# The leading expert is chosen four units early, half of its w1 is loaded during attention, and the gap between attention and experts is reordered

## The chip, the cores and the metric

The kernel runs on one NeuronCore of a Trainium2 chip. Its time is the device time of one execution in microseconds; the figure that counts is the median of the runs shown. The engines are called PE (TensorE), DVE (VectorE), ACT (ScalarE), POOL (GpSimd) and SP (SyncE, which mainly issues DMAs). Each engine works through its own instructions in order.

## The reference

Three stages follow each other. The first is a gated linear attention over 4 batches, 8 heads, 768 positions and 48 columns a head: `state = f * state + k v`, `y = q state`, with `f = sigmoid(f_logit)`. The second is a mixture of 8 experts with one expert a token; the third is a gated two-matrix product and two more matrices.

```python
# x: 3072 tokens x 384, from the attention
xn = x / (norm(x) + 1e-6);  en = emb / (norm(emb) + 1e-6)
logits = xn @ en.T / tau
expert_idx = argmax(logits, axis=1)
gate_w = softmax(logits)[arange(N), expert_idx]
for e in range(8):
    mask = expert_idx == e
    out[mask] = gate_w[mask, None] * (relu(x[mask] @ w1[e]) @ w2[e])   # w1[e] 384x1024, w2[e] 1024x384
# then
h = (out @ g1) * (out @ g2) @ g3
return h @ g_out
```

## The kernel before

**Attention and routing.** The 3072 tokens are 24 units of 128 (6 chunks of 4 batches). Attention is a software pipeline over units, written out by hand in the list `parts` (from L748), and each engine executes its instructions in the order in which the program states them. For each unit `s_xt` makes the token-major output and partial logits on PE, `s_sq` the sum of squares on ACT, `s_lg` (L534) the logits on DVE. `route(u0, n)` (L571) routes n units: GpSimd takes a power for the norm (L582), DVE finds the expert of each token (L583 to L594), PE counts its rank among that expert's tokens (matmuls L599 to L602, with the running counts `base`), DVE makes the row to write to (L612), the norm and the softmax denominator (L613 to L622), and GpSimd scatters each unit with one indirect DMA (L626) into `xsd`, 3072 rows for each expert. Route calls cover 6, 6, 4 and 4 units during attention (the list `routing`), then three (`pre`) and one (`last`) behind it.

**Choosing the order of experts.** `finish_route()` (L635, called `ends`) runs after all 24 units: PE sums the counts (`cnt`, L642) and a flag (`ok`, L643), and DVE ranks the experts by count (L651 to L677). Slot 0 is the expert with the most tokens. The results are `slot_e` (the expert of each slot), `slot_r` (its row in `xsd`) and `offs` (its columns in the result). SyncE reads `slot_e` and `slot_r` into registers to address loads. Slot by slot the matmuls have the fixed widths 448, 428, 416, 404, 396, 388, 384 and 376 columns.

**The gap.** Behind the attention loop comes a stretch (L790 to L833) in which the last two units and the routing end on DVE, while PE gets other work: part of the product of g3 and g_out for the third stage. `w3_turn(i)` transposes a tile of g3 on PE (L166), ACT and DVE evacuate it into two parts (L168, L169); `w3_times(i)` makes 24 products of 384 columns (L177) in four steps of six, and ACT and DVE copy the result out (L180, L181). `turn_w` and `times_w` hold four such tiles as generators, and `step(gen, n)` issues their next n steps, so the order of the calls in the gap is the order on every engine.

**The experts.** A phase is half an expert: half of w1 (768 KB) and half of w2. `prefetch(ph)` loads both into the two `stg` buffers (L306), whose memory attention used before, and lists their splits (ACT L134, GpSimd or DVE L135: upper and lower part) for `wsplit`. In phase 0 the w1 half is loaded on SyncE's queue, the w2 half on ScalarE's. `xs_load(0)` (L848) gathers the rows of slot 0 after the last scatter, `xs_gate` scales them with the gate (L865 on DVE, L867 on ACT), `xs_prep` transposes them (L876), and `g1_step` and `g2_step` are the expert's matmuls (L889, `hb`, and L903, `acc`), the first of which ends the gap. The third stage (L985, L998) follows when the experts are done.

Of the kernel before, what the change touches and what calls it, by code (L numbers as in the profile page):

```python
# [19 lines left out]
def attn_moe_glu_kernel(  # L20
# [61 lines left out]
    slot_r = const.tile([P, E], I32, name="slot_r")  # L82
    didx = const.tile([P, NU], I32, name="didx")
# [11 lines left out]
    cvw = [None]  # L95

# [205 lines left out]
    def fetch(ph, src, shape, q=SP):  # L302
        h = ring[ph % 2].tile(shape, F32R, tag="wh", name="wh")
        l = ring[ph % 2].tile(shape, F32R, tag="wl", name="wl")
        t = stage[0].tile(shape, F32, tag="stg", name="stg")
        q.dma_start(out=t, in_=src)  # L306
# [7 lines left out]
    def phase_src(ph, i, q):  # L314
# [4 lines left out]
        e = q.value_load(slot_e[0:1, n:n + 1], min_val=0, max_val=E - 1)  # L319
# [7 lines left out]
    def prefetch(ph):  # L327
        ta, ga = fetch(ph, phase_src(ph, 0, SP), [P, KD, 512])
        wsplit.add(ga)
        yield  # L330

        q = SP if ph else A
        tb, gb = fetch(ph, phase_src(ph, 1, q), [P, 4, DM] if ph < 2 * E else [P, KD, 512], q)
        phases[ph] = (ta, tb)
        wsplit.add(gb)
# [231 lines left out]
    def route(u0, n):  # L567
# [12 lines left out]
        pi = t1("pi", I32)  # L580
# [53 lines left out]

    def finish_route():  # L635
# [5 lines left out]
        b, b2 = bank([P, E], "cnt"), bank([P, 1], "ok")  # L641
# [13 lines left out]
        V.tensor_tensor(out=key, in0=key, in1=num, op=ALU.subtract)  # L655
# [24 lines left out]
    with tc.manual_schedule():  # L680
# [37 lines left out]
        def constants():  # L718
            V.tensor_copy(out=num, in_=slot_e)
            for dst, a, b in ((wrev, -1.0, E), (cbase, N, 0), (base, N // P, 0)):  # L720
                V.tensor_scalar(out=dst, in0=num, scalar1=float(a), scalar2=float(b), op0=ALU.mult, op1=ALU.add)
            for e in range(E):
# [69 lines left out]
        step(routing[-1], 2)  # L792
# [5 lines left out]
        s_lg(NU - 2)  # L798
        pre = route(NU - 4, 3)
        last = route(NU - 1, 1)  # L800
        ends = finish_route()
        step(pre)
# [3 lines left out]
        step(times_w[0], 2)  # L806
        spread.append(1)
        step(pre, 7)
        s_xt(NU - 1)
        s_sq(NU - 1)  # L810
        step(times_w[0])
        s_lg(NU - 1)
# [3 lines left out]
        step(ends)  # L816
        step(last, 5)
        step(times_w[1])
        step(last)
        step(times_w[1])  # L820
        step(last)
        step(ends, 2)
        for _ in range(3):
            step(last)
            step(ends)
        step(last, 99)
        step(ends, 99)
        step(times_w[0], 9)
        step(times_w[1])
        step(turn_w[2], 9)  # L830
        step(times_w[1], 9)
        attn.close()
# [12 lines left out]
        def xs_load(e):  # L845
            r = SP.value_load(slot_r[0:1, e:e + 1], min_val=0, max_val=(E - 1) * N)
# [63 lines left out]
        step(ahead)  # L910
        xs_load(0)
        step(turn_w[3], 9)
        step(times_w[2], 2)
        wsplit.pull(3)
        step(ahead)
# [8 lines left out]
        close_w3()  # L924
# [242 lines left out]
```

## Time and profile before

| | us |
|---|---|
| median of 3 runs | 738.99 (738.5 to 739.14) |
| the profiled execution | 736.44 |
| its span, first to last instruction | 734.7 |
| TensorE busy | 717.3 |
| VectorE, ScalarE, GpSimd busy | 345.4, 337.5, 339.2 |
| mean granted TensorE clock | 0.995 of full |

The rows of the trace are timed from the start of the span of the profiled execution, which is 1.7 us shorter than that execution. Matmuls are pipelined and their ends are modelled: of a run of matmuls the start of the next thing says more than the busy time. A timeline row gives start, duration, engine, line, what is written and read, how many were merged into the row, and in brackets the idle time before it and what ended that.

### The profile page before, as it was taken

The page shows a single profiled execution, that of the slowest core. Times are in us where ns is not written, and L with a number is a line of the kernel's source. Part 1 is how long each engine was busy: PE and PEld are TensorE (multiplying, and loading weights), DVE is VectorE, ACT ScalarE, POOL GpSimd, SP SyncE. Part 2 cuts the span into 40 slices and gives each one's busy share as a digit, 9 for nine tenths or more (in the row PEclk, how much of TensorE's full clock was granted, in tenths as well). Part 3 has the DMA queues.
Part 4 walks back from the last instruction along what each step waited for, and adds up shares of the span by engine and source line. Part 5 has one row for each costly group of instructions (what it writes and reads, how often), then busy time and mean ns, then how long its engine had stood idle before and what let it go on. Part 6 is the DMA issues. An engine that isn't in the chain of part 4 may idle for free.

```text
span 734.7 us, 13343 instructions
## 1 busy us (share of the span) xinstructions
PE 717.3 (98%) x5169; PEld 657.9 (90%) x5169; DVE 345.4 (47%) x672; ACT 337.5 (46%) x703; POOL 339.2 (46%) x423
## 2 busy tenths in 40 slices
PE   8999999998999999999999999999999999999996
PEld 7999989988999899999999988988888888888885
DVE  8889999956455564345343132222322322323222
ACT  5687978844557475465554542122112122121210
POOL 5467787783977776584564852102202201221002
PEclk9999999999999999999999999999999999999998
DMA  8999999626767778645443230000100100100001
GB/s 165 237 215 222 228 249 231 168 99 189 239 195 244 217 237 259 189 145 153 133 136 106 97 86 1 22 22 1 43 1 1 43 1 1 43 1 22 22 1 46
DMA packets 132158, 86.50 MB, mean 118 GB/s; under 512 B 106481, under 2 KB 114681, under 8 KB 132089
## 3 DMA queue, kind: packets, MB, share of 16 engines
q1 hardware_dynamic: 128489, 75.34, 38.6%
q0 software_dynamic: 3072, 9.46, 3.5%
q8 instruction: 42, 0.69, 0.4%
q10 hardware_dynamic: 528, 0.79, 0.4%
q14 instruction: 27, 0.22, 0.1%
HBM read 70.57 MB, written 15.01 MB: 116 GB/s over the span
## 4 chain that ended last, share of the span: by engine, by line
PE 54%; issue 10%; DMA 5%; POOL 4%; ACT 2%; DVE 1%; SPq 1%; POOLq 0%; ACTq 0%; DVEq 0%
PE pa L985 11%; PE pb L985 11%; PE ob L998 10%; PE acc L903 9%; PE hb L889 9%; DMA stg<-in_moe_w_dram 5%; PE wpb L177 4%; POOL wl L135 1%; POOL out_dram L1005 1%; DMA gd<-gt 1%; ACT wh L134 1%; PE xb L876 1%; POOL gt L222 1%; POOL x L135 0%; PE w3b L166 0%
## 5 line engine op out<-in xcount | busy, mean ns | idle before, releaser
L135 POOL TENSOR_TENSOR wl<-stg,wh 128x384 fp32r<-128x384 f32 (+1 forms) x121 | 139.1, 1179 | 64.2 <-ACT wh L134 64.2
L988 DVE TENSOR_TENSOR a<-a,pb 128x512 f32<-128x512 f32 x48 | 33.0, 688 | 181.6 <-PE pb L985 175.5
L998 PE MATMUL ob<-wp,ab 128*128 128x384 f32 x576 | 108.2, 339 | 0.0
L998 PEld LDWEIGHTS ob<-wp,ab 128*128 128x128 f32 x576 | 102.3, 188 | 3.8
L903 PE MATMUL acc<-h,wh 128*128 128x448 f32 (+7 forms) x384 | 104.1, 351 | 1.0 <-DVE h L892 0.5
L889 PE MATMUL hb<-xT,wh 128*128 128x448 f32 (+7 forms) x384 | 102.5, 348 | 0.0
L985 PE MATMUL pa<-x,wh 128*128 128x512 f32 x288 | 90.2, 394 | 0.0
L985 PE MATMUL pb<-x,wh 128*128 128x512 f32 x288 | 89.9, 393 | 0.0
L892 DVE SCALAR_TENSOR_TENSOR h<-hb,h 128x448 fp32r<-128x448 f32 (+7 forms) x64 | 37.0, 579 | 108.6 <-ACT h L891 108.3
L987 ACT COPY a<-pa 128x512 f32<-128x512 f32 x48 | 28.2, 587 | 120.6 <-PE pa L985 120.6
L1005 POOL DMA_INDIRECT out_dram<-o,didx x24 | 23.2, 965 | 129.4 <-DVE o L1004 126.0
L135 POOL TENSOR_TENSOR x<-xd,x 128x512 fp32r<-128x512 f32 x18 | 22.8, 1293 | 120.6 <-ACT x L134 120.6
L990 ACT CAST ab<-a 128x512 fp32r<-128x512 f32 x48 | 29.8, 620 | 104.7 <-DVE a L988 104.7
L134 ACT CAST wh<-stg 128x384 fp32r<-128x384 f32 (+1 forms) x124 | 62.7, 563 | 32.5 <-DMA stg<-in_moe_w_dram 26.6
L903 PEld LDWEIGHTS acc<-h,wh 128*128 128x128 f32 x384 | 70.4, 188 | 4.3 <-ACT h L891 1.5
L889 PEld LDWEIGHTS hb<-xT,wh 128*128 128x128 f32 x384 | 70.8, 188 | 1.4
L889 PE MATMUL hb<-xT,wl 128*128 128x448 f32 (+7 forms) x192 | 66.7, 348 | 0.0
L903 PE MATMUL acc<-h,wl 128*128 128x448 f32 (+7 forms) x192 | 66.7, 347 | 0.0
L985 PEld LDWEIGHTS pb<-x,wh 128*128 128x128 f32 x288 | 54.2, 188 | 12.7
L985 PEld LDWEIGHTS pa<-x,wh 128*128 128x128 f32 x288 | 53.6, 188 | 9.2
L891 ACT ACTIVATE h<-hb 128x448 fp32r<-128x448 f32 (+7 forms) x64 | 32.4, 507 | 62.5 <-PE hb L889 61.8
L985 PE MATMUL pb<-x,wl 128*128 128x512 f32 x144 | 56.9, 395 | 0.0
(185 smaller groups left out, 1276.0 us busy)
## 6 DMA issues: line engine op xcount, KB each, us to landing
stg<-in_moe_w_dram SPq DMA_DIRECT2D x31, 768.0 KB, 5.8
raw<-in_moe_w_dram SPq DMA_DIRECT2D x28, 512.0 KB, 5.6
xs<-xsd SPq DMA_DIRECT2D x8, 675.5 KB, 7.4
q<-in_q_dram SPq DMA_DIRECT2D x24, 192.0 KB, 5.0
k<-in_k_dram SPq DMA_DIRECT2D x24, 192.0 KB, 5.2
v<-in_v_dram SPq DMA_DIRECT2D x24, 192.0 KB, 4.5
f<-in_f_logit_dram SPq DMA_DIRECT2D x23, 192.0 KB, 4.4
raw<-in_moe_w_out_dram SPq DMA_DIRECT2D x8, 384.0 KB, 4.6
```

What stands on the lines that cost most here:

```text
L134: A.copy(out=hi, in_=src)
L135: eng.tensor_tensor(out=lo, in0=src, in1=f32(hi), op=ALU.subtract)
L177: PE.matmul(out=o, lhsT=t[:, x, j, :], rhs=wo[:, y, j, :], start=(j + n == 0), stop=(j == KF - 1 and n == 2))
L889: PE.matmul(out=b, lhsT=w[x][:, kk, cs], rhs=xT[e][y][:, kk, :], start=(kk + n == 0), stop=(kk == KD - 1 and n == 2))
L891: A.activation(out=h[0], in_=b, func=AF.Relu)
L892: V.scalar_tensor_tensor(out=h[1], in0=b, scalar=0.0, in1=f32(h[0]), op0=ALU.max, op1=ALU.subtract)
L903: PE.matmul(out=acc[d], lhsT=w[x][:, s % 4, d * P:(d + 1) * P], rhs=hs[s][y], start=(s + n == 0), stop=(s == KF - 1 and n == 2))
L985: PE.matmul(out=b, lhsT=w[x][:, kk, cs], rhs=x2[n][y][:, kk, :], start=(kk + m == 0), stop=(kk == KD - 1 and m == 2))
L988: V.tensor_tensor(out=t, in0=t, in1=pb, op=ALU.mult)
L990: A.copy(out=ab[s][0], in_=t)
L998: PE.matmul(out=oacc[t], lhsT=ab[s][x][:, t * P:(t + 1) * P], rhs=wp[:, y, s, :], start=(s + m == 0), stop=(s == KF - 1 and m == 2))
L1005: ins = G.indirect_dma_start(out=out, out_offset=bass.IndirectOffsetOnAxis(ap=didx[:, j:j + 1], axis=0), in_=o, in_offset=None,)
```

## The change

- `choose()` (called `lead`) takes the counts after 20 units with one matmul and finds the expert that leads. Ten small DVE instructions write its number and its row into `first`, and `numc`, which `finish_route` now takes for ties, puts that expert into slot 0 whatever the last four units bring.
- The w1 half of phase 0 goes into a buffer of its own, `w1s`, and its load is issued as soon as `first` is there, in the middle of the gap. The w2 half of phase 0 and the gather of slot 0 are addressed from `first` too, the w2 half now on SyncE's queue.
- In `route`, `pi` has six buffers instead of two. The counts `cnt` and `ok` go to the other PSUM pool.
- The order of the gap is new: the last two scatters of `routing[-1]` stand behind the first step of `pre`; w3 products and the steps of `last` and `ends` alternate in another way; two steps of `times_w[2]` stand ahead of `turn_w[3]`.

```diff
@@ -80,6 +80,8 @@
     win = const.tile([P, E], F32, name="win")
     slot_e = const.tile([P, E], I32, name="slot_e")
     slot_r = const.tile([P, E], I32, name="slot_r")
+    numc = const.tile([P, E], F32, name="numc")
+    first = const.tile([P, 2], I32, name="first")
     didx = const.tile([P, NU], I32, name="didx")
     xsd = dram.tile([E * N, XW], F32, name="xsd")
     xg = dram.tile([N, DM], F32, name="xg")
@@ -93,6 +95,9 @@
     cv = cvx.enter_context(tc.tile_pool(name="cv", side="right", bufs=1, reuse_waits="tile"))
     wo = cv.tile([P, 2, KF, DM], F32R, name="wo")
     cvw = [None]
+    pre_pool = ExitStack()
+    early = pre_pool.enter_context(tc.tile_pool(name="early", side="right", bufs=1, reuse_waits="tile"))
+    w1s = early.tile([P, KD, 512], F32, name="w1s")
 
     def open_w3(tiles, turns):
         cvw[0] = tc.tile_pool(name="cvw", side="right", bufs=1, reuse_waits="tile")
@@ -299,11 +304,12 @@
     ring = []
     stage = []
 
-    def fetch(ph, src, shape, q=SP):
+    def fetch(ph, src, shape, q=SP, t=None):
         h = ring[ph % 2].tile(shape, F32R, tag="wh", name="wh")
         l = ring[ph % 2].tile(shape, F32R, tag="wl", name="wl")
-        t = stage[0].tile(shape, F32, tag="stg", name="stg")
-        q.dma_start(out=t, in_=src)
+        if t is None:
+            t = stage[0].tile(shape, F32, tag="stg", name="stg")
+            q.dma_start(out=t, in_=src)
 
         def gen():
             for i in range(shape[1]):
@@ -316,7 +322,7 @@
         half_f = slice(hf * 512, (hf + 1) * 512)
         if n == E:
             return gd[i][:, half_f].rearrange("(k p) f -> p k f", p=P)
-        e = q.value_load(slot_e[0:1, n:n + 1], min_val=0, max_val=E - 1)
+        e = q.value_load(slot_e[0:1, n:n + 1] if n else first[0:1, 0:1], min_val=0, max_val=E - 1)
         if i == 0:
             return w1[bass.ds(e, 1), :, half_f].rearrange("o (k p) f -> p (o k) f", p=P)
         return w2[bass.ds(e, 1), half_f, :].rearrange("o (k p) d -> p (o k) d", p=P)
@@ -325,12 +331,10 @@
     wsplit = Background()
 
     def prefetch(ph):
-        ta, ga = fetch(ph, phase_src(ph, 0, SP), [P, KD, 512])
+        ta, ga = fetch(ph, phase_src(ph, 0, SP), [P, KD, 512]) if ph else fetch(0, None, [P, KD, 512], t=w1s)
         wsplit.add(ga)
         yield
-
-        q = SP if ph else A
-        tb, gb = fetch(ph, phase_src(ph, 1, q), [P, 4, DM] if ph < 2 * E else [P, KD, 512], q)
+        tb, gb = fetch(ph, phase_src(ph, 1, SP), [P, 4, DM] if ph < 2 * E else [P, KD, 512])
         phases[ph] = (ta, tb)
         wsplit.add(gb)
 
@@ -577,7 +581,7 @@
         r0, rinv = t1("r0"), t1("rinv")
         nb = rt.tile([P, E], F32, name="nb", bufs=2)
         t, sm = t8("t"), t1("sm")
-        pi = t1("pi", I32)
+        pi = rt.tile([P, 8], I32, name="pi", bufs=6)[:, 0:n]
         flat = lambda a: a.rearrange("p g e -> p (g e)")
         G.tensor_tensor(out=r0, in0=ssq[:, us], in1=half[:, 0:1].to_broadcast([P, n]), op=ALU.pow)
         V.tensor_reduce(out=mx, in_=L, axis=AX.X, op=ALU.max)
@@ -632,13 +636,36 @@
             scatters.append(ins)
             G.memset(half[:, 1:2], 0.0)
 
+    def choose():
+
+
+        b = bank([P, E], "lead", "acc")
+        PE.matmul(out=b, lhsT=ones, rhs=base)
+        yield
+        key, hot, t = [rt.tile([P, E], F32, name=n) for n in ("lkey", "lhot", "lt")]
+        s = rt.tile([P, 2], F32, name="ls")
+        V.scalar_tensor_tensor(out=key, in0=b, scalar=float(E), in1=numc, op0=ALU.mult, op1=ALU.subtract)
+        yield
+        V.tensor_reduce(out=s[:, 0:1], in_=key, axis=AX.X, op=ALU.max)
+        yield
+        V.tensor_scalar(out=hot, in0=key, scalar1=s[:, 0:1], scalar2=None, op0=ALU.is_equal)
+        yield
+        V.tensor_tensor(out=t, in0=hot, in1=num, op=ALU.mult)
+        V.tensor_scalar(out=hot, in0=hot, scalar1=float(2 * E * N), scalar2=None, op0=ALU.mult)
+        yield
+        V.tensor_reduce(out=s[:, 1:2], in_=t, axis=AX.X, op=ALU.add)
+        V.tensor_tensor(out=numc, in0=num, in1=hot, op=ALU.subtract)
+        yield
+        V.tensor_copy(out=first[:, 0:1], in_=s[:, 1:2])
+        V.tensor_scalar(out=first[:, 1:2], in0=s[:, 1:2], scalar1=float(N), scalar2=None, op0=ALU.mult)
+
     def finish_route():
         okb = rt.tile([P, 1], BF16, name="okb")
         low = rt.tile([P, 1], F32, name="low")
         V.tensor_reduce(out=low, in_=pend.rearrange("p u j -> p (u j)"), axis=AX.X, op=ALU.min)
         V.tensor_scalar(out=okb, in0=low, scalar1=1e-18, scalar2=None, op0=ALU.is_ge)
         yield
-        b, b2 = bank([P, E], "cnt"), bank([P, 1], "ok")
+        b, b2 = bank([P, E], "cnt", "acc"), bank([P, 1], "ok", "acc")
         PE.matmul(out=b, lhsT=ones, rhs=base)
         PE.matmul(out=b2, lhsT=ones, rhs=okb)
         yield
@@ -652,7 +679,7 @@
         yield
         V.tensor_scalar(out=key, in0=cnt, scalar1=float(E), scalar2=None, op0=ALU.mult)
         yield
-        V.tensor_tensor(out=key, in0=key, in1=num, op=ALU.subtract)
+        V.tensor_tensor(out=key, in0=key, in1=numc, op=ALU.subtract)
         yield
         V.tensor_tensor(out=gt, in0=rows(key), in1=cols(key), op=ALU.is_gt)
         yield
@@ -719,6 +746,7 @@
             V.tensor_copy(out=num, in_=slot_e)
             for dst, a, b in ((wrev, -1.0, E), (cbase, N, 0), (base, N // P, 0)):
                 V.tensor_scalar(out=dst, in0=num, scalar1=float(a), scalar2=float(b), op0=ALU.mult, op1=ALU.add)
+            V.tensor_scalar(out=numc, in0=num, scalar1=float(E * N + 1), scalar2=None, op0=ALU.mult)
             for e in range(E):
                 G.memset(win[:, e:e + 1], float(WIN[e]))
 
@@ -789,46 +817,62 @@
                 step(turn_w[i - NU], 2)
         for gen in routing[:-1]:
             step(gen, 99)
-        step(routing[-1], 2)
         s_xt(NU - 2)
         s_sq(NU - 2)
         step(times_w[0])
         s_inter(NU - 1)
         s_out(NU - 1)
         s_lg(NU - 2)
+        lead = choose()
         pre = route(NU - 4, 3)
         last = route(NU - 1, 1)
         ends = finish_route()
+        step(lead)
         step(pre)
         step(routing[-1], 99)
         spread.append(0)
         step(pre, 6)
-        step(times_w[0], 2)
+        step(times_w[0])
         spread.append(1)
-        step(pre, 7)
+        step(pre)
+        step(lead, 3)
+        step(pre)
         s_xt(NU - 1)
         s_sq(NU - 1)
         step(times_w[0])
+        step(lead)
+        step(pre)
+        step(lead)
+        step(pre)
+        step(lead, 9)
+        step(pre)
+        SP.dma_start(out=w1s, in_=phase_src(0, 0, SP))
+        step(pre)
         s_lg(NU - 1)
         step(last)
         step(pre, 99)
         spread.append(0)
-        step(ends)
         step(last, 5)
-        step(times_w[1])
+        step(times_w[0])
         step(last)
-        step(times_w[1])
-        step(last)
-        step(ends, 2)
-        for _ in range(3):
-            step(last)
-            step(ends)
-        step(last, 99)
-        step(ends, 99)
         step(times_w[0], 9)
         step(times_w[1])
+        step(ends)
+        step(last)
+        step(ends)
+        step(last)
+        step(turn_w[2])
+        for _ in range(2):
+            step(ends)
+            step(last)
+        step(times_w[1])
+        step(ends)
+        step(last, 99)
         step(turn_w[2], 9)
+        step(times_w[1], 2)
+        step(ends, 3)
         step(times_w[1], 9)
+        step(ends, 99)
         attn.close()
         open_psum(5, 3)
 
@@ -843,7 +887,7 @@
         ids_of = {}
 
         def xs_load(e):
-            r = SP.value_load(slot_r[0:1, e:e + 1], min_val=0, max_val=(E - 1) * N)
+            r = SP.value_load(slot_r[0:1, e:e + 1] if e else first[0:1, 1:2], min_val=0, max_val=(E - 1) * N)
             xst[e] = m1p.tile([CAP // 4, 4, XW], F32, name="xs")
             SP.dma_start(out=xst[e], in_=xsd[bass.ds(r, CAP), :].rearrange("(p c) w -> p c w", c=4))
 
@@ -907,12 +951,11 @@
                     V.tensor_copy(out=xd[:, d, bass.ds(o, WIN[e])], in_=acc[d])
 
         ahead = prefetch(0)
-        step(ahead)
+        step(ahead, 2)
         xs_load(0)
+        step(times_w[2], 2)
         step(turn_w[3], 9)
-        step(times_w[2], 2)
         wsplit.pull(3)
-        step(ahead)
         step(times_w[2], 9)
         for c in range(4):
             xs_gate(0, c)
@@ -922,6 +965,7 @@
         wsplit.pull(2)
         step(prefetch(1), 2)
         close_w3()
+        pre_pool.close()
         xd = moe.enter_context(tc.tile_pool(name="xd", reuse_waits="tile", bufs=1)).tile([P, KD, DENSE], F32, name="xd")
         open_w3(2, 1)
         bg.add(late())
```

## Rows read from the trace of the kernel before

**Rows 1.** The page: busy us (share of span) of each engine.
```profile
PE 717.3 (98%) x5169; PEld 657.9 (90%) x5169; DVE 345.4 (47%) x672; ACT 337.5 (46%) x703; POOL 339.2 (46%) x423
```

**Rows 2.** TensorE's waits, 181 to 734 us: total, times, longest.
```profile
PE acc L903 <- DVE h L892: 0.5, 3, 0.2
PE acc L903 <- ACT h L891: 0.4, 1, 0.4
```

**Rows 3.** TensorE's waits in the gap, 150 to 185 us.
```profile
PE w3b L166 <- DVE w3t L169: 2.2, 1, 2.2
PE rk L599 <- DVE oh L592: 0.8, 1, 0.8
PE wpb L177 <- DVE wp L181: 0.4, 1, 0.4
```

**Rows 4.** Timeline of TensorE, 150 to 200 us.
```profile
155.37 2.36 PE L177 MATMUL wpb<-wo,w3t 128*128 128x384 f32 x12
157.66 0.93 PE L524 MATMUL xl<-sel,yT 128*64 128x104 f32 x16
158.53 2.37 PE L177 MATMUL wpb<-wo,w3t 128*128 128x384 f32 x12
161.66 0.18 PE L599 MATMUL rk<-oh,tri 128*128 128x8 bf16 x1 [0.76 <-DVE oh L592]
...
168.79 0.66 PE L166 MATMUL w3b<-ident,g 128*128 128x128 f32 x4 [2.21 <-DVE w3t L169]
169.85 8.10 PE L177 MATMUL wpb<-wo,w3t 128*128 128x384 f32 x36 [0.41 <-DVE wp L181]
177.79 1.31 PE L876 MATMUL xb<-ident,xs 112*128 112x112 f32 x12
...
181.04 0.57 PE L889 MATMUL hb<-xT,wh 128*128 128x448 f32 x2
```

**Rows 5.** Stretches of 0.5 us; PEclk is the first figure after the engines.
```profile
170.00:170.50 0.50, 0.50 (x3) 0.50 (x4) 0.50 (x2) 0.07 (x1) 0.00 (x0) 0.79 0.94 332
...
171.00:171.50 0.50, 0.50 (x3) 0.50 (x2) 0.00 (x0) 0.00 (x0) 0.00 (x0) 0.50 1.06 414
...
173.50:174.00 0.50, 0.50 (x4) 0.50 (x4) 0.00 (x0) 0.50 (x2) 0.31 (x1) 0.80 0.74 173
```

**Rows 6.** Timeline of VectorE, 143 to 161 and 160 to 200 us.
```profile
158.84 0.17 DVE L613 TENSOR_SCALAR r<-r 128x3 f32<-128x3 f32 x1 [2.89 <-POOL r L582]
...
160.23 0.16 DVE L534 TENSOR_REDUCE lg<-xl 128x8 f32<-128x32 f32 x1
...
165.34 0.16 DVE L622 RECIPROCAL xt<-sm 128x1 f32<-128x1 f32 x1
...
168.05 1.28 DVE L169 TENSOR_TENSOR w3t<-w3b,w3t 128x512 fp32r<-128x512 f32 x2
```

**Rows 7.** Timeline of GpSimd, 155 to 205 us.
```profile
155.62 0.96 POOL L626 DMA_INDIRECT xsd<-xt,pi  x1 [0.19 <-issue]
...
157.89 0.91 POOL L582 TENSOR_TENSOR r<-ssq,half 128x3 f32<-128x3 f32 x1
...
166.27 0.96 POOL L626 DMA_INDIRECT xsd<-xt,pi  x1 [0.72 <-POOL half L633]
```

**Rows 8.** Weight-half loads (tile stg), 160 to 200 us, issue to landing.
```profile
DMA to landing us min/median/max: 4.6/4.7/5.0
```

**Rows 9.** Timeline of SyncE's queue, 155 to 215 us.
```profile
167.95 0.40 SPq L306 DMA_DIRECT2D stg<-in_moe_w_dram  x1
169.49 0.35 SPq L848 DMA_DIRECT2D xs<-xsd  x1
```

**Rows 10.** Scatters (L626), 150 to 170 us, issue to landing.
```profile
DMA to landing us min/median/max: 2.7/3.0/4.2
```

**Rows 11.** Gathers of an expert's rows (L848), whole kernel.
```profile
DMA to landing us min/median/max: 4.8/7.4/7.5
```

**Rows 12.** Timeline of ScalarE, 160 to 200 us.
```profile
176.28 1.12 ACT L867 ACTIVATE xs<-xs 112x384 f32<-112x384 f32 x2
```

## The prediction

> **What bounds the kernel now.** I read the engines' busy time first. TensorE is busy for 717.3 of 734.7 us [rows 1], so time is to be had only where TensorE stands still or runs slowly. Next I read its waits. From 181 us to the end of work it waits 0.9 us in all [rows 2]; in the gap between attention and experts, 150 to 185 us, it waits 2.2 us for a VectorE evacuation of a transposed w3 tile (L169), 0.8 us for a one-hot (L592) and 0.4 us for L181: 3.4 us [rows 3]. No weight load and no gather stands in that list.
>
> TensorE's timeline shows where [rows 4]. The 0.76 us lie before the rank matmul of the last unit (161.66 us), the 2.21 us in the middle of `turn_w[3]` (168.79 us), the 0.41 us before a run of 36 w3 products (169.85 us). That run is also slow: it takes 8.10 us, and 12 such products earlier take 2.37 us, so 36 should take 7.1. The granted clock says why: it is 0.50 of full, the lower of the two levels (1.2 GHz), from about 170.3 to 173.7 us, right behind the two waits [rows 5]. That is 1.0 us more. **The change can win at most 3.4 + 1.0 = 4.4 us in the gap.**
>
> VectorE's queue shows the cause of the long wait. The two evacuations L169 of `turn_w[2]` stand at 168.05 us, behind the whole of the routing's end [rows 6], while TensorE had run out of work at 166.6. And VectorE had lost time itself: the three-unit route `pre` waited 2.89 us for GpSimd's power (L582), which began at 157.89 us, behind the last two scatters of the group before, the first of them at 155.62 [rows 6, 7].
>
> **The change, part by part.**
>
> *Which expert goes first.* Counted from the reference's inputs (seed 0), expert 7 leads after 20 units with 352 tokens (the next has 342) and at the end with 417 (405). So the order of experts, the windows and the matmul columns stay as they are: 0 us.
>
> *choose().* One bf16 matmul with 8 columns: its like at 161.66 us is 0.18 us long [rows 4] and overlaps its neighbours; taken as 0.05, bounds 0 and 0.18. Ten small VectorE instructions: a chain of such goes at about 0.2 us each, since from r at 158.84 to the logits at 160.23 it is 1.4 us for seven steps, one on ScalarE among them [rows 6]. Most of choose's ten fall in pauses of that chain, the others make it longer: 0.5 us, bounds 0 and 2.0. The one operation for `numc`, early in attention, lies beside TensorE work: 0, bound 0.2.
>
> *The two scatters moved behind pre's power.* The power can start when the scatter before 155.62 ends, so at about 155.5 instead of 157.89 us: 2.4 us earlier. With choose's 0.5 us, the last unit's logits (L534, at 160.23, right behind pre's reciprocal) come at 158.3; their product is ready by then, as six w3 products go in front of it where twelve went (157.66 less 1.2). The two scatters themselves go later, on a queue that has room: the last unit's scatter, at 166.27, waits for its own reciprocal (165.34), not for them [rows 4, 6, 7].
>
> *New order of the gap.* The last unit's chain from logits to reciprocal takes 5.1 us now. In the new order one L181 and one L169 (about 0.6 us each by the pair at 168.05) and the two instructions on `pend` stand in it, and a wait for its own power, which now stands earlier in GpSimd's queue, goes: about 6.0 us. The reciprocal comes at 164.3 instead of 165.34, the last scatter, 0.8 us behind as now, at 165.1 instead of 166.27. In return the count's matmul, which now follows six products of `times_w[1]`, waits for `base`: from pre's rank matmul at 155.3 TensorE has 24 products at 0.19 us and the 16 matmuls of s_xt, 0.9 us, and ends at 160.9 or 161.0; `base` is the eighth small step behind the logits, with L181 and `pend` in between: 161.5. So a new wait of 0.6 us (bounds 0 and 1.5). The evacuations of `turn_w[2]` no longer stand behind the end of routing, and twelve products of `times_w[2]` stand in front of `turn_w[3]`: the waits of 2.2 and 0.4 us go, and with them the lower clock. I take all 4.4 us as gone and 0.6 as new.
>
> *w1's half loaded early, w2's half behind it.* Both loads go out on SP once `first` is there, at some 158.5 and 159.4 us; a load takes 4.6 to 5.0 us [rows 8], so they are in by 165. Nobody on TensorE waited for them, so this alone gives 0. What it does is clear the way of xs_load(0): now it is issued at 169.49, 1.5 us behind the w1 load in the same queue [rows 9]. After, it goes when the last scatter has landed, which takes 3.0 us by the median of the gap's ten [rows 10] and 3.2 for this one (166.27 to 169.49): at 168.3. Its own landing takes 4.8 to 7.5 us where the trace has it [rows 11]. I take 4.8, the case nearest in kind: that gather had a free queue ahead of it and loads only behind. Landed at 173.1. The w1 load of phase 1 now follows right behind xs; since it goes second I charge it nothing, and 7.5 us is the other bound. ScalarE's two gates start at 176.28 and take 1.1 us [rows 12]. In the new order TensorE has, from the count at 161.65, 54 products at 0.19 us and 16 transposes (four take 0.66 us alone, less in a row; 2.0 us taken) and reaches xs_prep at 174.0; the gates end at 174.4: a wait of 0.4 us (bounds 0, and 3.1 with the 7.5 us).
>
> *Other edits.* w2's issue leaves ScalarE's queue; pi has six buffers, as its scatters run later; cnt and ok move to the other PSUM pool: 0, all beside TensorE work; if the cover failed, one such issue on a queue, 0.4 us, is the largest [rows 9]. The order of the other experts (slot_e, slot_r, offs) comes ready at about 169 us and is first read for expert 1, tens of us later.
>
> **Sum.** Gone 3.4 + 1.0; new 0.6 + 0.4 + 0.05. The first expert matmul comes 3.35 us earlier, at 177.7 instead of 181.04 [rows 4], and since TensorE is full behind it [rows 2], so does the end. Profiled execution: 736.44 - 3.35 = 733.1 us. The median of the runs shown is 2.55 us above that execution, so 738.99 - 3.35 = **735.6 us**. What a measurement of this kernel can tell from no change is about 0.2%, 1.5 us.
>
> **The rivals.**
>
> *Partial (0.13): the w2 load is not early.* Its buffer lies where attention's tiles were. If it becomes free only when attention ends, at about 167.5, the load is issued just ahead of xs, as w1 is now. Then xs, issued at 168.4, has a load in front of it and lands near 175, the gates end at 176.1, and TensorE waits 2.1 us at xs_prep instead of 0.4: 1.7 us won, 737.3. Against it: by the order of allocation the buffer lies on q tiles, which are last read long before.
>
> *No change (0.18): the wait only moves.* Either xs takes the 7.5 us of its longest landing: 175.8, gates to 177.0, TensorE idle for 3 us and then, as in [rows 5], 1.0 us lost at the lower clock; or VectorE, which holds choose, both chains and the evacuations in one queue, still releases a w3 bank 2 to 3 us late; or the expert stage's own loop of loads and splits is a limit. 3.35 less 2.7 or more leaves 0 to 0.7: 738.3 to 739. For it: the median landing of xs is 7.4 [rows 11]. Against the loop: only 0.9 us of waits behind 181 us [rows 2].
>
> *Slower (0.09): the early loads hold up the scatters.* From 158.5 us 1.5 MB of weights and the last six scatters are in flight together. Scatters in the gap land in 2.7 to 4.2 us [rows 10]; xs waits for the last one. If that one takes as long as a gather's longest, 7.5 us, xs goes at 172.6 and lands at 177.4, the gates end at 178.6, 0.8 us after the present xs_prep (177.79), and 4 us of waiting put the lower clock on what follows, 1.0 us: 738.99 + 1.8 = 740.8. The point from which it decides is a landing above 5.7 us, where xs_prep comes 1.0 us early and loses that at the lower clock. Against it: both loads should be in before 165.1, when the last scatter starts. The Trainium skill's page "DMA: Bandwidth & Descriptors" (section "Issuing engines are not separate DMA queues") speaks for this rival: DMAs started by the sync and gpsimd engines end on the same 16 DMA engines and interleave, whichever engine started them. By that rule the scatters that go from 159 to 164 us are slowed for certain; in the trace no scatter of the gap runs beside a weight load except the end of the last, so it does not show by how much.
>
> **How the numbers follow.** The forecast has 0.60, with 734.3 to 737.0 as its own range: 734.6 with all 4.4 us, a little below if the 0.9 us later shrink; 737.0 if the new waits cost 1.4 us more. Partial 0.13, no change 0.18, slower 0.09. The range reaches from 734.3 to 738.4 and leaves out the slower case and most of the unchanged one. Faster by over 0.2% (below 737.5): 0.60 and half of the partial case, 0.67. Within: the rest of that and nearly all of the unchanged case, 0.22. Slower: 0.11, with what of the unchanged case goes past the bound.
>
> **What would show it.** Right: no TensorE wait on L169 or L181 above 0.3 us, the clock at full from 165 to 180 us, w1 and w2 issued before 161, the last scatter at 165 to 165.5, xs issued near 168.4, the first hb matmul at 177 to 178.2, the expert stage unchanged. Wrong: a wait over 1 us at xs_prep or at the count's matmul, a span at 0.50 clock, or w2's issue after 166. If the end does not follow the first hb matmul, the expert stage has a limit of its own.

## The result and the profile after

The changed kernel is slower: a median of 744.31 us over 8 executions (740.71 to 745.91) against 739.07 (735.76 to 741.45) for the kernel before, ratio 1.0069 with a 95% interval of 1.0042 to 1.0095. The forecast, 735.6 us, lies on the other side, and the range ended at 738.4. The profiled execution took 743.41 us, its span 741.4 at a mean clock of 0.992.

**The engines' busy time of the page after** differs little from [rows 1]:

```profile
PE 716.4 (97%) x5170; PEld 657.2 (89%) x5170; DVE 351.5 (47%) x682; ACT 337.6 (46%) x703; POOL 339.8 (46%) x423
```

TensorE has no more work than before, so the 6.7 us that the span grew are waits. **The waits of TensorE after, from 150 to 190 us** (total, times, longest), show which of the gap's old ones are gone:

```profile
PE xb L920 <- ACT xs L911: 1.9, 1, 1.9
PE xl L528 <- ACT yT L486: 1.7, 1, 1.7
PE cnt L669 <- DVE base L613: 0.4, 1, 0.4
```

The waits on L169 (now L174), L181 and L592 of [rows 3] are not there. New are 0.4 us at the count's matmul and 1.9 us at xs_prep (`xb`). The wait of `xl` is one of attention. So the gap is no longer than before. **TensorE's timeline after** shows where it lies:

```profile
164.53 1.04 PE L481 MATMUL y<-am,v 128*64 128x128 f32 x16
...
171.76 0.17 PE L669 MATMUL cnt<-base,ones 128*128 128x8 bf16 x1 [0.44 <-DVE base L613]
...
178.74 4.42 PE L182 MATMUL wpb<-wo,w3t 128*128 128x384 f32 x24
185.03 1.77 PE L920 MATMUL xb<-ident,xs 112*128 112x112 f32 x12 [1.88 <-ACT xs L911]
...
190.22 0.57 PE L933 MATMUL hb<-xT,wh 128*128 128x448 f32 x2
```

and the same view of the kernel before has this row for the last unit's product:

```profile
154.28 1.04 PE L477 MATMUL y<-am,v 128*64 128x128 f32 x16
```

The last unit's product marks the end of attention. It starts at 154.28 us before and at 164.53 after: **10.25 us later**. From there to the first hb matmul the kernel before takes 26.76 us [rows 4], the changed one 25.69. From hb to the end of the span it is 553.7 and 551.2 us. So 10.25 - 1.07 - 2.5 = 6.7 us, and what made the kernel slower is in attention, whose work the change hardly touches (one instruction for `numc`, more buffers for `pi`). The last term is not read: over the fifteen profiles of this study hb to the end varies from 551 to 556 us. Most of that lies in the second to fourth expert: from the first matmul of the second to the first of the fifth it is 87.5 to 92.6 us (89.6 before, 88.2 after), while the first expert takes 30.5 us in all fifteen.

**Attention's stretches of 50 us** (busy PE, PEld, DVE, ACT, POOL; then clock, share of the DMA engines, GB/s) before:

```profile
0.00:50.00 50.00, 46.03 (x611) 41.97 (x613) 43.42 (x98) 34.21 (x77) 25.82 (x66) 1.00 0.95 203
50.00:100.00 50.00, 49.27 (x774) 45.67 (x775) 46.49 (x96) 40.71 (x99) 39.73 (x61) 1.00 0.97 230
100.00:150.00 50.00, 49.11 (x778) 45.04 (x778) 47.77 (x115) 40.57 (x99) 38.27 (x60) 1.00 0.84 201
```

and after:

```profile
0.00:50.00 50.00, 41.84 (x555) 37.67 (x557) 40.24 (x91) 30.28 (x68) 23.74 (x63) 1.00 1.12 183
50.00:100.00 50.00, 48.30 (x749) 44.30 (x747) 44.62 (x93) 40.94 (x101) 35.35 (x54) 1.00 1.03 213
100.00:150.00 50.00, 47.34 (x735) 43.86 (x729) 45.64 (x101) 35.25 (x84) 37.81 (x59) 0.97 1.07 229
```

In the first stretch fewer bytes move (183 against 203 GB/s) while the DMA engines are busier (1.12 against 0.95; shares over 1 mean that the records of packets overlap). So the transfers take longer. **The DMA issues of the first 25 us** (count, KB each, median us to landing) before:

```profile
q<-in_q_dram SPq DMA_DIRECT2D x6, 192.0 KB, 3.6
k<-in_k_dram SPq DMA_DIRECT2D x6, 192.0 KB, 3.6
f<-in_f_logit_dram SPq DMA_DIRECT2D x6, 192.0 KB, 3.7
```

and after:

```profile
k<-in_k_dram SPq DMA_DIRECT2D x6, 192.0 KB, 5.1
f<-in_f_logit_dram SPq DMA_DIRECT2D x6, 192.0 KB, 5.3
q<-in_q_dram SPq DMA_DIRECT2D x5, 192.0 KB, 4.9
```

**ScalarE's waits for loads, 0 to 150 us,** before and then after (`f` is a gate; `raw` are weights of the third stage, converted during attention):

```profile
ACT g L256 <- DMA raw<-in_moe_w_dram: 5.3, 4, 1.9
ACT gt L256 <- DMA raw<-in_moe_w_out_dram: 5.1, 4, 1.6
...
ACT f L401 <- DMA f<-in_f_logit_dram: 4.4, 4, 1.6
```

```profile
ACT gt L261 <- DMA raw<-in_moe_w_out_dram: 9.6, 4, 4.6
ACT g L261 <- DMA raw<-in_moe_w_dram: 7.4, 3, 4.3
ACT f L405 <- DMA f<-in_f_logit_dram: 6.9, 7, 2.9
```

Together they grow from 14.8 to 23.9 us, and what stands behind them in ScalarE's order waits with them.

**The theory (A).** The tiles q, k, f and v have rows of 64 floats of which a load fills 48. Each load therefore writes runs of 192 bytes at steps of 256, each a packet of its own in the trace: 24 units x 4 tensors x 128 partitions x 8 heads = 98,304 packets. The two new tiles in the pool `const`, `numc` (32 bytes in a partition) and `first` (8, which take up 32), move everything allocated behind them by 64 bytes. The first q tile began at byte 44,352 of a partition, 64 past a multiple of 256, and now begins at 44,416, 128 past. A run of 192 bytes from 64 ends exactly at the next multiple of 256; one from 128 crosses it. **The rivals:** (B) the new order, the early loads, the counts' other pool or the buffer `early` reach back into attention; (C) chance, from where a program's data happen to lie.

The trace's record of every packet gives a direct reading. The mean duration of these 98,304 packets is 15.58 ns before, with 1.0% above 15 ns, and 19.29 ns after, with 28.8% above; the median is 15 ns in both. The last of them starts at 141.5 us before and at 151.5 after, 10 us later, as the last unit's product does. Packets of 2048 bytes, of which 9,216 are in each trace, are not slower: 96.3 ns before, 93.7 after.

### The profile page after: what moved, and what is told of

Its sections match the earlier page's. It is cut to its first block, busy times and chain, and to the rows that moved or that the text cites. A ratio compares the mean times of both kernels' runs of the same rounds, so it can differ in the third digit from the quotient of the medians.

```text
span 741.4 us, 13350 instructions
## 1 busy us (share of the span) xinstructions
PE 716.4 (97%) x5170; PEld 657.2 (89%) x5170; DVE 351.5 (47%) x682; ACT 337.6 (46%) x703; POOL 339.8 (46%) x423
## 4 chain that ended last, share of the span: by engine, by line
PE 68%; DMA 8%; issue 8%; SPq 4%; ACT 4%; POOL 4%; DVE 3%; POOLq 0%; ACTq 0%; DVEq 0%
PE acc L947 12%; PE hb L933 12%; PE pa L1029 11%; PE pb L1029 11%; PE ob L1042 11%; SPq L382 3%; PE wpb L182 3%; DMA stg<-in_moe_w_dram 2%; DMA raw<-in_moe_w_dram 2%; DMA f<-in_f_logit_dram 1%; PE xl L528 1%; DMA raw<-in_moe_w_out_dram 1%; PE y L473 1%; PE y L481 1%; PE a L446 1%
## 5 line engine op out<-in xcount | busy, mean ns | idle before, releaser
L140 POOL TENSOR_TENSOR wl<-stg,wh 128x384 fp32r<-128x384 f32 (+1 forms) x119 | 136.5, 1178 | 58.9 <-ACT wh L139 58.9
L140 POOL TENSOR_TENSOR x<-xd,x 128x512 fp32r<-128x512 f32 x18 | 22.8, 1289 | 119.9 <-ACT x L139 119.9
L139 ACT CAST wh<-stg 128x384 fp32r<-128x384 f32 (+1 forms) x121 | 61.1, 562 | 27.1 <-DMA stg<-in_moe_w_dram 21.1
L1029 PE MATMUL pa<-x,wl 128*128 128x512 f32 x144 | 57.1, 396 | 0.0
```

What stands on the lines that cost most here:

```text
L139: A.copy(out=hi, in_=src)
L140: eng.tensor_tensor(out=lo, in0=src, in1=f32(hi), op=ALU.subtract)
L1029: PE.matmul(out=b, lhsT=w[x][:, kk, cs], rhs=x2[n][y][:, kk, :], start=(kk + m == 0), stop=(kk == KD - 1 and m == 2))
```

## The experiments

The table gives the start of the last unit's product, the gap (from there to the first hb matmul), both from one profile, the mean packet, and the median beside that of the kernel before on the same chip, with the ratio and its interval. "Offset" is where the q, k, f and v tiles begin, modulo 256 bytes. The ratio is given as it was measured with its interval; it is not the quotient of the two medians. Each profile is of one execution, and not always of a typical one: b_fv64's took 740.86 us and b_rest64's 741.25, the longest of their ten, b_qk64's 734.87, the shortest. So the two columns of times scatter from profile to profile.

| run | offset | last product | gap | packet ns | median us | before | ratio |
|---|---|---|---|---|---|---|---|
| before | 64 | 154.28 | 26.76 | 15.58 | | | |
| after | 128 | 164.53 | 25.69 | 19.29 | 744.31 | 739.07 | 1.0069 [1.0042, 1.0095] |
| b_pad64 | 128 | 166.00 | 27.15 | 19.85 | 746.26 | 737.40 | 1.0117 [1.0076, 1.0158] |
| b_pad128 | 192 | 164.63 | 26.98 | 20.10 | 746.45 | 737.11 | 1.0112 [1.0077, 1.0147] |
| b_pad192 | 0 | 154.43 | 26.06 | 15.52 | 735.99 | 737.40 | 1.0000 [0.9971, 1.0030] |
| a_pad192 | 64 | 156.03 | 23.29 | 15.46 | 737.11 | 737.40 | 0.9989 [0.9963, 1.0015] |
| a_pad128 | 0 | 157.23 | 23.64 | 15.47 | 736.58 | 737.40 | 0.9982 [0.9955, 1.0009] |
| b_early | 0 | 155.66 | 26.38 | 15.47 | 737.28 | 737.21 | 0.9999 [0.9978, 1.0020] |
| b_fv64 | f, v 128 | 158.11 | 26.97 | 15.90 | 738.61 | 737.21 | 1.0017 [0.9996, 1.0038] |
| b_qk64 | q, k 128 | 153.70 | 26.44 | 16.18 | 737.73 | 737.16 | 1.0017 [0.9995, 1.0039] |
| b_ld64 | all four 128 | 162.95 | 26.19 | 19.88 | 745.33 | 737.16 | 1.0124 [1.0079, 1.0168] |
| b_rest64 | 64, the rest moved | 157.08 | 27.14 | 15.45 | 735.55 | 737.16 | 0.9991 [0.9964, 1.0018] |
| order_only | 0 | 156.73 | 28.49 | 15.5 | 740.05 | 737.11 | 1.0034 [1.0015, 1.0053] |
| early_only | 0 | 155.42 | 27.42 | 15.5 | 738.97 | 737.11 | 1.0018 [0.9996, 1.0040] |
| w2_late | 0 | 155.72 | 23.30 | 15.5 | 735.55 | 737.11 | 0.9983 [0.9963, 1.0002] |

**The bytes alone, without the change: b_pad64 and b_pad192.** One line in the kernel before, behind `slot_r`; the tile is never used. b_pad192 has 48 in place of 16.

```diff
+    pad = const.tile([P, 16], F32, name="pad")
```

> The kernel before with one unused 64-byte tile more per partition among the constants, so that attention's tiles for q, k, v and f start where those of the changed kernel start: 128 instead of 64 bytes past a multiple of 256, so that a run of 192 bytes crosses such a multiple. Theory A (the new constants moved the tiles, and the 192-byte runs of attention's loads became slower): the products of the last unit come 7 to 10 us later than in before, the 192-byte packets take a mean of about 19 ns instead of 15.6, and the time is 743 to 749. Theory B (the new order, the early loads or the new buffer on the other side slow attention): nothing changes, 739 within 1.5. Theory C (chance, where a program's data happen to lie): no relation to the tiles.

> The kernel before with 192 unused bytes more, so that attention's tiles start at a multiple of 256 and no run crosses one. Theory A: as before or a little better, 736 to 739.5, mean of the 192-byte packets 15 to 16 ns. Theory A in another form (any shift disturbs): as with 64 bytes. Theory B: 739 within 1.5.

Sixty-four unused bytes cost 1.17%; 192 cost nothing that shows (1.0000, interval 0.9971 to 1.0030). **TensorE's longest wait in b_pad64, 0 to 150 us,** is the one that the changed kernel has there too:

```profile
PE kb L459 <- ACT yT L483: 6.9, 3, 4.1
```

In the changed kernel that row reads

```profile
PE kb L462 <- ACT yT L486: 7.7, 5, 3.4
```

and in the kernel before

```profile
PE kb L458 <- ACT yT L482: 1.4, 4, 0.6
```

**The change with the tiles moved back: a_pad192 and a_pad128.** The same line in the changed kernel, with 48 and with 32.

> The changed kernel with 192 unused bytes more, so that attention's tiles start 64 bytes past a multiple of 256, as in before. Theory A: attention ends as early as in before, the products of the last unit near 154 us instead of 164.5, and what the gap gives shows: 734 to 738. Theory B: 744 within 2.

> The changed kernel with 128 unused bytes more, so that attention's tiles start at a multiple of 256. Theory A: within 1.5 of the one with 192 bytes, 734 to 738. Theory B: 744 within 2.

**TensorE's wait from above, in a_pad192:**

```profile
PE kb L463 <- ACT yT L487: 1.2, 3, 0.6
```

Attention is back at 156 to 157 us and the loss is gone, which leaves nothing of its size to (B). The gap is now 23.3 and 23.6 us, 3.1 to 3.5 shorter than before's 26.76 and 2.4 to 2.8 shorter than b_pad192's 26.06. **TensorE's timeline of a_pad192:**

```profile
156.03 1.04 PE L482 MATMUL y<-am,v 128*64 128x128 f32 x16
...
162.83 0.18 PE L604 MATMUL rk<-oh,tri 128*128 128x8 bf16 x1 [1.23 <-DVE oh L597]
...
171.04 4.42 PE L183 MATMUL wpb<-wo,w3t 128*128 128x384 f32 x24
175.33 0.32 PE L921 MATMUL xb<-ident,xs 112*128 112x112 f32 x1
175.97 1.41 PE L921 MATMUL xb<-ident,xs 112*128 112x112 f32 x11 [0.32 <-DVE xs L910]
...
179.32 0.57 PE L934 MATMUL hb<-xT,wh 128*128 128x448 f32 x2
```

The wait at the count's matmul is not there; one of 1.23 us at the one-hot takes its place.

**A fourth offset: b_pad128.** The kernel before with 32 in the line.

> The kernel before with 128 unused bytes more among the constants: attention's tiles start 192 bytes past a multiple of 256, so that runs of 192 bytes again cross one, at another place than with 64 bytes more. If the crossing is what costs: 744 to 749 like with 64 bytes, mean of the 192-byte packets 18 to 20 ns. If only the offset of 128 is bad: 736 to 740 and 15.5 ns.

Offsets 0 and 64 are alike, 128 and 192 are alike and slow. That is what runs that do or do not cross a multiple of 256 give, and not a matter of alignment to 128 bytes. Every second of these multiples is one of 512 as well; the four offsets do not tell whether both kinds cost.

**The buffer `early` alone: b_early.** b_pad192 with the pool and the tile `w1s`, unused.

```diff
+    pre_pool = ExitStack()
+    early = pre_pool.enter_context(tc.tile_pool(name="early", side="right", bufs=1, reuse_waits="tile"))
+    w1s = early.tile([P, KD, 512], F32, name="w1s")
```

> The kernel before with its tiles at a multiple of 256 (192 unused bytes), and the 6 KB buffer of the early w1 half allocated but not used, so that the w3 tiles lie 6 KB lower, as in the changed kernel. In all five variants with that buffer the last unit's products came at 155.4 to 157.2 us, in the two without it and with runs that cross nothing at 154.3 and 154.4. If the buffer's place costs attention 1 to 3 us: products at 155.4 or later, time 738 to 740. If that was chance from execution to execution: 154 to 155 us or anything up to 157 without a shift of the median, 736 to 738.5, as before within 0.3%.

0.9999: its place costs nothing that shows.

**Which tiles: b_fv64, b_qk64, b_ld64 and b_rest64.** Two unused tiles in the pool `ld` of the kernel before move some of its tiles by 64 bytes and those behind them by 256. For b_fv64 they stand around fs and vs, for b_qk64 around qs and ks, for b_ld64 around all four:

```diff
+    pad0 = ld.tile([P, 16], F32, name="pad0")
     qs = [ld.tile([P, H, 64], F32, name=f"q{i}") for i in range(NB)]
...
     vs = [ld.tile([P, H, 64], F32, name=f"v{i}") for i in range(NV)]
+    pad1 = ld.tile([P, 48], F32, name="pad1")
```

b_rest64 moves all that b_pad64 moves except those four: the const tile of 16, `pad0` of 48 and `pad1` of 16.

> The kernel before with only the tiles of f and v moved by 64 bytes, to 128 past a multiple of 256; q, k and all that is allocated outside attention's load tiles stay at their place modulo 64 bytes, and nothing of the experts moves. If the crossing runs of the loads are the cause, half of the loads cross: mean of the 192-byte packets about 17.5 ns, last unit's products 3 to 7 us later than in before, 740 to 744. If something else on the moved side is the cause (w3 products, expert tiles): as before, 736 to 738.5.

> The kernel before with the tiles of q and k alone moved by 64 bytes. With f and v alone moved, the time rose by 0.17% and the packets to 15.9 ns, less than half of the 1.2% and 19.8 ns of all. If the cost grows faster than the number of crossing runs (a queue that is full only when all cross): 737.5 to 740, 15.9 to 16.5 ns. If q and k are the ones that cost: 743 to 748 and 18 ns or more.

> The kernel before with the tiles of q, k, f and v alone moved by 64 bytes; the tile wp, from which the zeros are written to memory, and all else keep their place modulo 64 bytes. If the crossing runs of these four loads are the whole cause: as with everything moved, 744 to 748, mean of the 192-byte packets 19 to 20 ns. If another moved tile (wp as the source of the zero writes, the expert tiles) is the cause or a part of it: 736 to 742.

> The kernel before with everything on the left moved by 64 bytes except the tiles of q, k, f and v. If the four loads are the whole cause: as before, 736 to 738.5, packets 15.5 ns. If wp or the expert tiles take part: 740 or more.

b_ld64 has the whole cost (1.24%), b_rest64 none, so the four load tiles are the cause. Nor is it chance (C): in the four programs whose four tiles all cross, the last product comes at 163.0 to 166.0 us, in the eleven others at 153.7 to 158.1. Two of the four tiles measure 1.0017 each, with intervals that include 1, where I had expected of b_fv64 about half of the whole. The mean packet grows by 0.3 and 0.6 ns there, with all four by 4.3. **The DMA share in the stretches of attention, b_ld64:**

```profile
0.00:50.00 50.00, 44.07 (x535) 39.79 (x537) 39.33 (x88) 29.90 (x67) 23.61 (x62) 0.97 1.14 187
50.00:100.00 50.00, 50.00 (x799) 46.95 (x795) 45.89 (x97) 42.33 (x103) 36.33 (x57) 1.00 1.04 214
100.00:150.00 50.00, 45.37 (x710) 41.57 (x707) 45.61 (x100) 35.67 (x84) 37.01 (x57) 1.00 1.13 225
```

**b_fv64:**

```profile
0.00:50.00 50.00, 46.55 (x611) 42.21 (x613) 43.37 (x98) 34.18 (x77) 25.86 (x66) 1.00 0.98 203
50.00:100.00 50.00, 49.01 (x771) 45.33 (x771) 45.22 (x93) 38.35 (x95) 39.24 (x59) 1.00 0.96 225
100.00:150.00 50.00, 47.51 (x718) 43.91 (x720) 45.91 (x103) 39.83 (x97) 35.42 (x57) 0.97 0.86 202
```

With half of the runs crossing, the DMA engines move 203 and 225 GB/s in the first two stretches, near the 203 and 230 of before; with all, 187 and 214 at shares above 1. And crossing alone does not make a packet slow: with half crossing, 3.8 (b_fv64) and 6.7% (b_qk64) of all packets take more than 15 ns, with all crossing 29 to 38%. Why the time grows so much faster than the number of crossing runs, no run shows.

**The parts of the change: order_only and early_only.** Both start from a_pad128. order_only keeps the new order and drops choose(), the early loads and the use of `first`, and w2's half goes back to ScalarE's queue (an excerpt):

```diff
-        ta, ga = fetch(ph, phase_src(ph, 0, SP), [P, KD, 512]) if ph else fetch(0, None, [P, KD, 512], t=w1s)
+        ta, ga = fetch(ph, phase_src(ph, 0, SP), [P, KD, 512])
...
-        lead = choose()
...
-        SP.dma_start(out=w1s, in_=phase_src(0, 0, SP))
...
-        step(ahead, 2)
+        step(ahead)
         xs_load(0)
```

> The changed kernel with the tiles at a multiple of 256 and only the new order of the gap: no choose(), w1 and w2 of phase 0 loaded as in before (after slot_e, w2 on ScalarE's queue). Theory P (the order removes TensorE's waits for VectorE, the early loads are needed so that the gather of slot 0 lands in time): no wait on L169 or L181, but a wait of 2 to 3 us at xs_prep, and the gap from the last unit's products to the first expert matmul takes 25 to 26 us, against 26.1 to 26.8 in before and 23.3 to 23.6 in the changed kernel with shifted tiles; time within 0.3% of before. Rival Q (the order alone does it): 23.3 to 24 us, time 735 to 737.

early_only keeps choose() and the early loads, in the order of the kernel before (an excerpt):

```diff
+        step(routing[-1], 2)
         s_xt(NU - 2)
...
-        step(lead, 3)
-        step(pre)
+        step(lead, 9)
+        SP.dma_start(out=w1s, in_=phase_src(0, 0, SP))
+        step(pre, 6)
```

> The changed kernel with the tiles at a multiple of 256 and the old order of the gap, with choose() put in and the loads early. Theory P: TensorE waits 2 us for L169 and 0.4 us for L181 as before, the gather lands earlier and nobody gains: the gap takes 26 to 27 us, time within 0.3% of before. Rival (the loads are what gives): 24 us or less.

Neither part gains alone. In **order_only's timeline** the w1 load goes ahead of the gather on SyncE's queue

```profile
171.44 0.40 SPq L313 DMA_DIRECT2D stg<-in_moe_w_dram  x1
172.81 0.35 SPq L887 DMA_DIRECT2D xs<-xsd  x1
```

and TensorE, early, waits for it:

```profile
179.79 0.31 PE L915 MATMUL xb<-ident,xs 112*128 112x112 f32 x1 [4.14 <-ACT xs L906]
```

That is 4.1 us where I expected 2 to 3. The gap of 28.5 us, for which I had 25 to 26, is the longest of all, and the time is 0.34% over the kernel before. **early_only's waits in the gap** keep the old one on the w3 evacuation:

```profile
PE w3b L172 <- DVE w3t L175: 2.6, 1, 2.6
PE xl L529 <- ACT yT L487: 0.9, 1, 0.9
PE rk L604 <- DVE oh L597: 0.6, 1, 0.6
```

**w2 behind the gather: w2_late.** a_pad128 with w1 early and w2's load issued behind xs.

```diff
-        step(ahead, 2)
+        step(ahead)
         xs_load(0)
+        step(ahead)
```

> The changed kernel with the tiles at a multiple of 256, and the w2 half of phase 0 issued behind the gather of slot 0 instead of ahead of it. If the early loads hold up the scatters: the last scatter lands 0.5 to 1.5 us sooner after its start, the gather is issued and lands that much earlier, and the gap is up to 1 us shorter than 23.6 us. If they don't: the gap takes 23.3 to 23.9 us and the time is that of the changed kernel with shifted tiles, 736 to 737.5, within what can be told.

Its median is 735.55 against 737.11, its ratio that of a_pad128 (0.9983 and 0.9982), and its interval ends at 1.0002. From the start of its last scatter (166.65 us) to the issue of xs (169.65) it is 3.0 us; with w2 early it is 3.2 and 3.3 in the a_pad runs and 4.6 in the changed kernel. The gap, 23.30 us, is that of a_pad192 (23.29). So the scatters are held up by some 0.2 to 0.3 us at most by w2's early load in these profiles, and the differences among w2_late and the two a_pad runs are too small for a verdict.

## Why the prediction was wrong

**The step that failed** is the one called "Other edits", with the sentence on `numc` in "choose()" ("lies beside TensorE work: 0, bound 0.2"). I costed the new tiles by the instructions that write them. What they cost is their size: 64 bytes move the load tiles of attention to where each run of 192 bytes crosses a multiple of 256. That is 10.25 us of attention in the profile, and 8.2 us by the medians of b_ld64, which moves nothing else (745.33 - 737.16), where I had 0. In the changed kernel itself the ratios put it at 0.8 to 0.9% (1.0069 against 0.9989 and 0.9982), some 6 us. No rival held it either: none of the three was about attention, which I took as unchanged, and I read no row of its DMA engines. A share of 0.95, 0.97 and 0.84 over its three stretches leaves (0.05 + 0.03 + 0.16) x 50 = 12 us of room. The packets' extra time is (19.29 - 15.58) ns x 98,304 / 16 engines = 22.8 us. An estimate from both, 10.8 us late, is near the measured 10.25; for b_fv64 the extra time, (15.90 - 15.58) x 98,304 / 16 = 2.0 us, is well inside the room. How near it comes is luck: b_pad192, no slower than before, has shares of 1.01, 1.01 and 0.83, which leave 7.5 us by the same sum and would give 15.7. As records of packets overlap, such a share is not a measure of room, but one of 0.95 was reason enough to give attention a bound of its own and not a price of 0.

The Trainium skill's page "DMA: Bandwidth & Descriptors" (section "How a descriptor splits into AXI transactions") says that a transaction starts at a multiple of 256 bytes, and that a descriptor which does not start at one has its first transaction start at the boundary below. It tells this of what a transaction reads; here the offsets are those of the tiles that the loads write. Worked out by its rule, as an estimate, 192 bytes from 128 or 192 need two transactions and from 0 or 64 one. The runs agree on which offsets are slow. By the same rule 64 would need more beats than 0, 8 against 6; there the runs show no difference (15.58 and 15.52 ns).

**Gone waits: right in the main.** In the changed kernel the waits on L169, L181 and L592 are gone, and so is the lower clock at 170 to 174 us. With the tiles put back the gap is 3.1 to 3.5 us shorter, where I forecast 3.35. Luck has a part in that: there the wait for the one-hot (L592 before, L597 now), which I had as gone, is 1.2 and 1.3 us, and against b_pad192 the gap is only 2.4 to 2.8 us shorter.

**Times in the gap, counted from the last unit's product:** the forecast had GpSimd's power at 1.2 us, the last unit's logits at 4.0, the reciprocal at 10.0, the last scatter at 10.8, xs's issue at 14.0, the end of the gates at 20.1, hb at 23.4. The changed kernel has 1.06, 3.85, 9.67, 10.10, 14.72, 20.95 and 25.69. Up to the scatter the forecast holds within 0.7 us. choose()'s 0.5 us (nine VectorE instructions, not ten) fits into that.

**The count's wait:** 0.44 us for a forecast of 0.6, in the changed kernel. In the a_pad runs it is not there; the last unit's logits come at 5.6 us, not 3.85, and the rank matmul waits 1.2 to 1.3 us. The row that makes them late is **ScalarE's in a_pad192**:

```profile
161.08 0.48 ACT L530 COPY xt<-xl 128x384 f32<-128x384 f32 x1 [2.12 <-remote]
```

The row names no releaser. By the trace's semaphore records the copy waits for the one that the last matmul of `xl` raises; it rises at 161.06 us, though that matmul's row ends at 159.3. In the changed kernel row and semaphore agree (167.8 us). Why they part here no run settled.

**xs_prep:** 1.9 us of wait in the changed kernel for a forecast of 0.4. Two things add up. TensorE comes there 18.6 us after the product (185.03 - 1.88 - 164.53), where I had 19.7. And the last scatter needs longer: xs is issued 4.62 us behind its start, where I took 3.2. **GpSimd's and SyncE's timelines after:**

```profile
174.63 0.96 POOL L630 DMA_INDIRECT xsd<-xt,pi  x1 [0.83 <-DVE xt L626]
```

```profile
168.98 0.40 SPq L849 DMA_DIRECT2D w1s<-in_moe_w_dram  x1
170.25 0.39 SPq L312 DMA_DIRECT2D stg<-in_moe_w_dram  x1
179.25 0.34 SPq L892 DMA_DIRECT2D xs<-xsd  x1
```

Behind this wait the clock falls, **in the stretch 186 to 189.5 us to a mean of 0.57:**

```profile
186.00:189.50 3.50, 3.50 (x17) 3.50 (x16) 1.69 (x3) 1.39 (x3) 0.00 (x0) 0.57 0.04 12
```

From 186.5 to 189.5 us it is 0.50, the lower of the two levels (1.2 GHz), and twelve w3 products take 3.90 us there, 1.5 more than the 2.36 of [rows 4]. So the mechanism of the rival "slower" is there in part. **The landing of the four scatters that start from 169.5 to 174.6 us, after,** is longer than in [rows 10]:

```profile
DMA to landing us min/median/max: 4.4/5.8/6.2
```

Yet the last one, which was to decide, takes 4.4 us and not 7.5. The crossing runs are not what slows it: b_pad64, with the same offsets and no early loads, issues xs 3.03 us behind the start of the last scatter (177.61 to 180.64). Nor do the early loads alone slow it, as the a_pad runs have them too and need 3.2 and 3.3. In the changed kernel the last scatter starts 4.4 us behind the issue of w2's load, in the a_pad runs 5.2; but early_only, also at 5.2, needs 4.33. What decides between 3.2 and 4.6 us stays open.

**"So does the end": open.** In the a_pad runs the gap is 3.1 to 3.5 us shorter, 0.45% of the time, but the ratios are 0.9989 and 0.9982, with intervals that include 1. In those profiles attention ends 1.8 and 3.0 us later than in the profile of before, in b_early, with an equal median, 1.4 later. From the second expert to the fifth they take 91.5 (a_pad192) and 90.5 us against 89.6, but b_rest64, without the change, takes 92.6. Single profiles can't tell such shifts from chance, and where the rest of the gain goes was not settled. At the same offset and on the same chip a_pad128 and b_pad192 have medians of 736.58 and 735.99 us, so no gain shows there. The intervals reach down to 0.9955: with its tiles in place the change is worth at most some 0.45%, and nothing is not excluded.

## What to carry to other kernels

A new tile costs more than the instructions that fill it: work out where the tiles allocated behind it come to lie, above all those that DMA fills in short runs, and give it a size, or a place behind them, that leaves their offsets as they were, or lets no run cross a multiple of 256. Before a stage is called untouched, look at what it is near the limit of: here the DMA engines had a share of 0.95 in attention's first stretch. And where two edits lean on each other (the order made TensorE early, the early load made its data early), run each alone: order_only is slower by 0.34%, early_only's ratio is 1.0018 with an interval that includes 1, and together they are at 0.9982 (0.9955 to 1.0009). Of these only order_only differs beyond its interval from the kernel before, and from both together.

## What the runs showed of the hardware that was not expected

- 98,304 packets of 192 bytes take 15.5 to 15.6 ns in the mean where their runs begin 0 or 64 bytes past a multiple of 256 in the partition, and 19.3 to 20.1 ns at 128 or 192. The median stays at 15 ns; 29 to 38% of the packets are slower instead of 1%.
- The cost is not proportional: with half of the runs crossing, the mean is 15.9 or 16.2 ns and the ratio 1.0017, with an interval that includes 1; with all, 19.9 ns and 1.24% more time. Even with all crossing, 62 to 71% of the packets take no more than 15 ns.
